# Half of the attention's statistics and transposes recorded with the convolutions, and copies by VectorE beside DMAs

## The chip, the cores and the metric

The kernel runs on one core of a Trainium2 chip. Its time is device microseconds of one execution, the median of several; lower is better. PE is TensorE, DVE VectorE, ACT ScalarE, POOL GpSimd, SP SyncE, which only issues DMAs. One more number goes with each run: the clock that was granted to TensorE, as a share of full speed.

## The reference

The input is x, 2048 positions of 512 channels in bfloat16. Four layers follow each other, each added to its input:

```
x = x + conv(layernorm(x))        # S4: one long filter per channel, made from A, B, C, log_dt; plus u * Dskip
x = x + attention(layernorm(x))   # 32 heads of 16; each position looks at 8 keys: its own and 7 earlier ones, 2 apart
x = x + conv(layernorm(x))        # the same filter
x = x + attention(layernorm(x))   # the same weights
```

The filter K[d, l] is the real part of a sum over 128 modes of C * exp(dt * A * l) * dt * B. The convolution is made with Fourier transforms of length 4096 and keeps the first 2048 outputs. The attention is x @ wqkv, logits against the 8 keys (masked before the start), softmax, a weighted sum of the 8 values, and wo.

## The kernel before

**X and its turned copy.** X stays in SBUF for the whole kernel as 128 partitions x 2 column halves x 16 rows x 256. Partition p, row j is position 16p + j; the column half (`h`, `cp`) is channels 0 to 255 or 256 to 511. A quarter `q` is four rows j. The attention's matmuls need channels on the partitions, so X is turned into XT (`turned_view(U)`, in the memory of U, which in the convolution layers holds the normalised input), in eight pieces: column half by quarter. A piece is turned by a DMA transpose from SP's queue or by eight PE transposes into `pt_x` and a copy on ACT or DVE (L1290, L1293, L1296).

**Statistics.** The attention's layer norm needs mean and variance of every row: DVE's `bn_stats` (L1348) on each half row of 256 elements, 32 a layer, into `pst`, then `bn_aggr` (L1352), joined per quarter, then ACT. Queries and keys are projected from XT without waiting for the statistics, whose scale enters later.

**Stages and orders.** There are four stages, each a `Plan`: the preparation, the filter and the first convolution (`kernel_and_first_conv`); the first attention (`b_layer`); the second convolution (`a_layer`); the second attention (`b_layer` again). A stage records its operations, each with an engine, a cost in us, its dependences and rings of buffers that it takes and drops. The cost plays no part at run time. `either` records several ways of doing one operation, for example a copy on ACT or on DVE. A list of numbers, `ORDERS[stage]`, worked out beforehand, says which way is taken and in which order all operations are issued:

```
order = [int(i) for i in ORDERS[Plan.turn].split()]
taken = {self.ops[i][2] for i in order}
```

Each engine works through its own share in that order, and waits by semaphores for other engines. An instruction that waits holds everything behind it on its engine.

**The first convolution.** Tables of powers of the modes (Xtab, Ytab) are built in 8 units by DVE (`table_ops`, L467 to L480), PE contracts them to the filter, and the filter (kind k) and the input (kind u) go through a Fourier transform in two steps, in four channel groups `dc` of 128 with four pieces `c` each. After the first step the spectrum Z is turned (`turn`: an SP DMA transpose into `zt`, or PE transposes into `pt` and an ACT copy, L912). After the second step, ACT's casts give sp_u and sp_k (L903). `swapped` makes a copy of sp_u with the two halves of the partitions exchanged, by two DMAs of 64 partitions x 1024 (L959), and `product` (`pa`, L966, DVE) multiplies sp_u and its exchanged copy by sp_k. `inverse` (`vp`, PE; `VT`) and `final` (`ps_y`, PE; X evacuated by ACT or DVE, L1006) go back, and add to X. sp_k is also stored to `kt_scratch` in DRAM for the second convolution.

**The second convolution** does the same for its input alone. `xc` is the spectrum; the filter comes back as `Kt`, a tile of 128 x 2 x 1024, whose two rows per partition are the partition's own and the one 64 away. `load` fills it by two DMAs of 64 x 2 x 1024, 256 KB each: those of dc 0 and 1 by POOL's queue, those of dc 2 and 3 by SP's (L1219). `pa` (L1169) multiplies both rows.

**The attention.** `start(q)` turns X and takes the statistics. `pair` and `qk` project queries and keys (`ps_qk`, L1409 and L1428; evacuated to qT, kT, L1433). `ahead` copies the last keys' columns to the front of kT (L1451) by SP's DMA, ACT or DVE. The products of queries and shifted keys are DVE's (L1508), the sums over a head are PE's (`Lp`, L1519). Then come softmax and, with the values (`ps_v`, L1463; VX), the products L1684, their sums on PE (L1700), and the output projection (`ps_o`, L1784) with X added.

Of the kernel before, what the change touches and what calls it, by code (L numbers as in the profile page):

```python
# [19 lines left out]
S = 2048  # L20
# [210 lines left out]
def load_params(nc, pp, prm):  # L231
# [307 lines left out]
def prepare(nc, pl, lp, pp, psA, psK, raw, identf, block, ones, M, cb, T, ln, X, D2, marks):  # L539
# [215 lines left out]
    marks["seeds"], marks["casts"] = o, casts  # L755


def kernel_and_first_conv(nc, tc, C, prm, x2d, const, kt_dram, eps, Wt):
    with ExitStack() as es:
        mt = es.enter_context(tc.tile_pool(name="k_mt", bufs=1))  # L760
        M = Multipliers(mt)
# [1200 lines left out]
```

## Time and profile before

| | |
|---|---|
| median of 3 runs | 442.48 us (439.23 to 443.36) |
| the profiled execution | 438.31 us, of which the span from first to last instruction is 436.5 us |
| mean granted TensorE clock | 0.986 |
| first convolution, with tables and filter | 0 to 165 us of the span |
| first attention | to about 276 us |
| second convolution | to about 326 us |
| second attention | to 436.5 us |

The stages overlap by a few microseconds at their borders. Busy times are sums of one engine's instructions in a stretch of the span. In the rows by group, the number ahead of the comma is the total busy time, the one behind it the mean duration of one instruction, then the idle time of that engine just before, and what ended it.

### The profile page before, as it was taken

What the parts mean: (1) busy time and instruction counts of PE and PEld (TensorE: products, weight loads), DVE (VectorE), ACT (ScalarE), POOL (GpSimd) and SP (SyncE); (2) the same over time, 40 slices, a digit from 0 to 9 for tenths busy, and PEclk for the clock granted to TensorE, in tenths of its full rate; (3) what the DMA queues carried; (4) which work ended last, traced back from release to release, by engine and by line L of the source; (5) the groups of instructions that cost most, each with busy time, mean ns of one, the idle gap of its engine ahead of it and who ended that gap; (6) DMA issues with size and microseconds to landing.
All of it is one profiled execution on the core that took longest, in us unless ns stands there. A gap on an engine that the chain in (4) does not pass through costs nothing.

```text
span 436.5 us, 11533 instructions
## 1 busy us (share of the span) xinstructions
PE 373.6 (86%) x4773; PEld 233.7 (54%) x4810; DVE 395.3 (91%) x659; ACT 320.6 (73%) x523; POOL 31.6 (7%) x94
## 2 busy tenths in 40 slices
PE   1376877788799988999997899898979999998995
PEld 1242665675587764446643344577754336743452
DVE  6999999799989479999899999998779999999994
ACT  6899999599789774677842578998855588853331
POOL 1000000000000410010000520010000010000150
PEclk9999899899899999999999999999999999999999
DMA  8977197789939988011213597299982000223296
GB/s 223 188 207 259 63 186 163 138 164 192 172 70 191 184 210 170 12 38 47 76 49 72 123 228 133 40 185 222 203 151 50 36 2 2 83 85 63 43 156 173
DMA packets 107306, 55.13 MB, mean 126 GB/s; under 512 B 85341, under 2 KB 97774, under 8 KB 106998
## 3 DMA queue, kind: packets, MB, share of 16 engines
q1 hardware_dynamic: 103990, 49.08, 53.4%
q0 software_dynamic: 2976, 5.06, 6.1%
q8 instruction: 37, 0.61, 0.6%
q10 hardware_dynamic: 288, 0.26, 0.2%
q14 instruction: 15, 0.12, 0.1%
HBM read 20.34 MB, written 6.29 MB: 61 GB/s over the span
## 4 chain that ended last, share of the span: by engine, by line
PE 38%; DVE 13%; DMA 6%; issue 2%; ACT 2%; SPq 0%; DVEq 0%; ACTq 0%
PE po L1700 7%; PE ps_qk L1409 6%; PE ps_v L1463 6%; PE ps_qk L1428 6%; DVE prod L1684 4%; PE Lp L1519 4%; PE ps_o L1784 3%; DVE prod L1508 2%; DMA oT<-ot 2%; DMA zt<-Z 2%; DMA Kt<-kt_scratch 2%; DVE pa L1169 1%; PE vp L1181 1%; PE ps_y L1202 1%; DVE ln_st_a L199 1%
## 5 line engine op out<-in xcount | busy, mean ns | idle before, releaser
L1684 DVE TENSOR_TENSOR prod<-VX,L 128x512 bf16<-128x512 bf16 (+2 forms) x72 | 75.5, 1102 | 2.0 <-ACT VX L1474 1.0
L1508 DVE TENSOR_TENSOR prod<-qT,kT 128x4096 bf16<-128x4096 bf16 (+1 forms) x40 | 72.1, 1861 | 1.8 <-ACT kT L1451 1.0
L1700 PE MATMUL po<-prod,sb_ident 128*128 128x512 bf16 x233 | 56.4, 379 | 2.8 <-DVE prod L1684 2.0
L1700 PEld LDWEIGHTS <-sb_ident 128*128 128x128 bf16 x240 | 23.1, 98 | 31.3 <-issue 4.1
L1463 PE MATMUL ps_v<-wv,U 128*128 128x256 bf16 x256 | 31.4, 273 | 0.6 <-ACT VX L1474 0.3
L1784 PE MATMUL ps_o<-wo_t,oT 128*128 128x512 bf16 x124 | 31.4, 379 | 0.4 <-ACT oT L1733 0.2
L875 ACT CAST Z<-ps_s 128x1024 bf16<-128x1024 f32 (+1 forms) x36 | 31.6, 952 | 0.0
L1474 ACT ACTIVATE VX<-ps_v,rs 128x256 bf16<-128x256 f32 x64 | 26.8, 474 | 6.0 <-PE ps_v L1463 5.6
L1409 PE MATMUL ps_qk<-U,wqk 128*128 128x512 bf16 x128 | 30.6, 380 | 0.3 <-ACT L L1647 0.3
L1718 ACT CAST ot<-po 128x1024 bf16<-128x1024 f32 (+1 forms) x16 | 15.1, 959 | 20.6 <-PE po L1700 20.6
L1428 PE MATMUL ps_qk<-U,wqk 128*128 128x512 bf16 x128 | 29.3, 379 | 0.0
L1463 PEld LDWEIGHTS <-U 128*128 128x128 bf16 x256 | 24.3, 98 | 8.9 <-issue 3.1
L966 DVE TENSOR_TENSOR pa<-sp_u,sp_k 128x2048 bf16<-128x2048 bf16 x16 | 19.6, 1222 | 7.9 <-DMA sp_u<-sp_u 4.3
L1519 PE MATMUL Lp<-prod,sb_bones 128*32 128x512 bf16 x256 | 22.9, 383 | 2.7 <-DVE prod L1508 2.7
L1348 DVE BATCH_NORM_STATS2 pst<-X 128x6 f32<-128x256 bf16 x64 | 21.9, 412 | 3.5 <-DMA sb_minus<-c_minus 2.6
L1169 DVE TENSOR_TENSOR pa<-xc,Kt 128x2048 bf16<-128x2048 bf16 x16 | 19.3, 1220 | 6.1 <-DMA Kt<-kt_scratch 4.1
L1409 PEld LDWEIGHTS <-wqk 128*128 128x128 bf16 x128 | 11.8, 98 | 16.8 <-issue 3.6
L1428 PEld LDWEIGHTS <-wqk 128*128 128x128 bf16 x128 | 12.2, 98 | 15.4 <-issue 1.6
L1784 PEld LDWEIGHTS <-oT 128*128 128x128 bf16 x128 | 12.2, 98 | 15.0 <-ACT oT L1733 0.7
L892 PE MATMUL xp<-zt,sb_C 128*128 128x512 bf16 x45 | 16.1, 411 | 4.3 <-DMA zt<-Z 1.4
L872 PE MATMUL ps_s<-KT,FK 128*128 128x128 bf16 (+1 forms) x360 | 18.3, 209 | 1.0 <-ACT KT L845 0.6
L1181 PE MATMUL vp<-sb_IC,pa 128*128 128x128 bf16 x256 | 16.3, 219 | 3.0 <-DVE pa L1169 2.7
(221 smaller groups left out, 841.3 us busy)
## 6 DMA issues: line engine op xcount, KB each, us to landing
sp_u<-sp_u SPq DMA_DIRECT2D x32, 128.0 KB, 3.0
kt_scratch<-sp_k SPq DMA_DIRECT2D x16, 256.0 KB, 3.9
Kt<-kt_scratch POOLq DMA_DIRECT2D x16, 256.0 KB, 7.7
Kt<-kt_scratch SPq DMA_DIRECT2D x16, 256.0 KB, 5.3
X<-in_A_u_dram SPq DMA_DIRECT2D x8, 256.0 KB, 5.6
X<-in_A_u_dram SPq DMA_DIRECT2D x4, 512.0 KB, 4.7
out_dram<-X SPq DMA_DIRECT2D x16, 128.0 KB, 2.0
VX<-VX SPq DMA_DIRECT2D x4, 448.0 KB, 3.7
```

Source lines behind the costliest of these rows:

```text
L875: nc.scalar.copy(box["Z", kind, dc, b0][:, 0:n // 4, :, jq * 16:(jq + 1) * 16].rearrange("p g r k -> p r g k"), box.pop(("s1", kind, dc, j ...
L1169: nc.vector.tensor_tensor(pr[:], x[:].unsqueeze(1).to_broadcast([128, 2, 1024]), box.pop(("kt", dc, c))[:], ALU.mult)
L1348: nc.vector.bn_stats(pst[:, j, cp, :], X[:, cp, j, :])
L1409: nc.tensor.matmul(ps[:], wqk[:, ct, f0:f0 + 128], XT[:, ct // 2, 4 * s:4 * s + 4, ct % 2, :], start=(ct == 0), stop=(ct == 3))
L1428: nc.tensor.matmul(box[name][:, k * 512:k * 512 + 512], wqk[:, ct, f0:f0 + 128], XT[:, ct // 2, 4 * s:4 * s + 4, ct % 2, :], start=(ct == ...
L1463: nc.tensor.matmul(ps[:, jj].rearrange("p t h d -> p (t h d)"), XT[:, ct // 2, j + jj, ct % 2, :], wv[:, ct, fp * 256:(fp + 1) * 256], sta ...
L1474: nc.scalar.activation(out, ps, ACT.Identity, scale=r)
L1508: nc.vector.tensor_tensor(pr[:], windows(q, 0, 2), windows(kT[fp][:, a:a + n2, col(w):col(w) + 1024], -DIL * 128, 2), ALU.mult)
L1519: nc.tensor.matmul(Lp[r0:r0 + 32, w // 4, :], bones[:, w % 4 + k, :], pr[:, k, f2 - a, hb * 512:(hb + 1) * 512], start=(n == 1 and k == 0) ...
L1684: nc.vector.tensor_tensor(p2[:].rearrange("p w j t d h -> p w (j t) d h"), windows(v, -DIL * 256, taps), l.to_broadcast([128, taps, nj * 2 ...
L1700: nc.tensor.matmul(po[:, c:c + 512], ident[:], p2[:, t, k + j:k + j + 2].rearrange("p j t d h -> p (j t d h)"), start=first, stop=stop)
L1784: nc.tensor.matmul(ps, oT[:, ft // 2, o:o + 128], wo_t[:, ft, :], start=(ft == 0 and not res), stop=(ft == 3))
```

## The change

- **Half 0 ahead.** A new function `ahead`, recorded at the end of both convolutions, turns column half 0 of X and takes its 16 half statistics within the convolution's plan. `start` of the attention keeps half 1. The other ways of making statistics (which the orders before did not take) are gone. U and `pst` are now allocated from the start, and the table X lies in U's memory until the contraction of unit 6 is done, so the transposes of half 0 in the first convolution wait for that.
- **Exchanged halves.** `swapped` may use two DVE copies of 64 partitions x 1024 instead of two DMAs. The new order takes them for 7 of the 16: (dc, c) = (0,2), (1,0), (2,0) and all of dc 3.
- **Kt copies.** `load` of dc 2 and 3 may fetch each row once, by two DMAs of 128 KB, and let DVE copy the other half of the tile, two copies of 64 x 1024. Taken for 7 of the 8, all but (3,1).
- **Turned spectra.** The copy of `pt` into `zt` may be DVE's too. Taken for five pieces in the second convolution.
- **Orders anew.** All four lists are replaced, so other ways are taken elsewhere as well. Over the kernel, DVE's instructions go from 661 to 689: 14 exchange copies and 14 Kt copies of 64 x 1024, 5 copies into zt and 3 more key copies are added; 3 casts of xc, 2 copies of pt_x, 3 subtractions on L and one addition on the value weights go. The DMAs in SP's queue go from 210 to 194. All eight pieces of half 0 are turned by SP's DMAs in the two convolutions; in the first attention two pieces of half 1 go by SP's DMA, one by ACT and one by DVE; in the second three by SP's DMA and one by ACT.

The core of the diff (orders and passed arguments left out):

```diff
-    def __init__(self, nc, tc, es, M):
+    def __init__(self, nc, tc, es, M, room):
...
-        self.X = pool.tile([128, UNIT, 2, NX, 2], BF, name="Xtab")
+        self.X = room[:].rearrange("p j d -> p (j d)").rearrange("n (h c e t) -> n h c e t", h=UNIT, c=2, e=NX)
...
+def ahead(pl, nc, X, XT, pst, psA, ident, ready, free, loaded):
...
+        def dma(js=js):
+            nc.sync.dma_start(XT[:, 0, js].rearrange("c j t p -> c (j t) p"), X[:, 0, js].rearrange("p j c -> p (j c)"), transpose=True)
...
+        pl.mark(("xt", q), pl.either(("turned", q), lambda: pl.op("S", 1.4, dma, ready[q], free, lag=3.2),
+                                     lambda: by_pe("A", 0.92, nc.scalar.copy), lambda: by_pe("V", 1.13, nc.vector.tensor_copy)))
+        pl.mark(("hs", q), *[pl.op("V", 0.34, lambda j=j: nc.vector.bn_stats(pst[:, j, 0, :], X[:, 0, j, :]), ready[q])
+                             for j in range(q * 4, q * 4 + 4)])
...
         def swapped(dc, c):
-            def swap():
+            def swap(move):
                 s = box["u", dc, c]
                 t = box["swap", dc, c] = box["xs"].pop(0)
                 for h in range(2):
-                    nc.sync.dma_start(box["U"][64 * h:64 * h + 64, t], box["U"][64 - 64 * h:128 - 64 * h, s])
...
+                    move(box["U"][64 * h:64 * h + 64, t], box["U"][64 - 64 * h:128 - 64 * h, s])
...
+                def once():
+                    k = box["kt", dc, c] = kp.tile([128, 2, 1024], BF, name="Kt", tag="Kt")
+                    for h in range(2):
+                        nc.sync.dma_start(k[64 * h:64 * h + 64, h], kt_dram[dc, c, 64 * h:64 * h + 64])
+
+                def other():
+                    k = box["kt", dc, c]
+                    for h in range(2):
+                        nc.vector.tensor_copy(k[64 - 64 * h:128 - 64 * h, h], k[64 * h:64 * h + 64, h])
...
+        ahead(pl, nc, X, turned_view(U), pst, psA, ident, [Xq[0, q] for q in range(4)], prev, [])
...
-            both = [turn(cp) for cp in range(2)]
-            ready = [r for r, _ in both]
-            turned[q] = [t for _, t in both]
...
+            turned[q] = [pl.outer(("xt", q)), turn()]
+
+            def half_stats(j):
+                nc.vector.bn_stats(pst[:, j, 1, :], X[:, 1, j, :])
```

More of the change, by code (lines that the diff above doesn't have):

```diff
@@ L755, in prepare, with mm, back_in, by_pe @@
     marks["seeds"], marks["casts"] = o, casts
-def kernel_and_first_conv(nc, tc, C, prm, x2d, const, kt_dram, eps, Wt):
+def ahead(pl, nc, X, XT, pst, psA, ident, ready, free, loaded):
+    box = {}
+    for q in range(4):
+        js = slice(q * 4, q * 4 + 4)
+        def dma(js=js):
+            nc.sync.dma_start(XT[:, 0, js].rearrange("c j t p -> c (j t) p"), X[:, 0, js].rearrange("p j c -> p (j c)"), transpose=True)
+        def mm(q=q):
+            pt = box[q] = psA.tile([128, 8, 128], BF, name="pt_x", tag="psA")
+            for k in range(8):
+                nc.tensor.transpose(pt[:, k, :], X[:, 0, q * 4 + k // 2, k % 2 * 128:k % 2 * 128 + 128], ident[:])
+        def back_in(copy, q=q, js=js):
+            copy(XT[:, 0, js], box.pop(q)[:].rearrange("c (j t) p -> c j t p", j=4))
+        def by_pe(eng, us, copy, q=q, mm=mm, back_in=back_in):
+            key = ("psA", "x", q)
+            return pl.op(eng, us, lambda: back_in(copy), free, pl.op("P", 0.5, mm, ready[q], loaded, take=key), drop=key)
+        pl.mark(("xt", q), pl.either(("turned", q), lambda: pl.op("S", 1.4, dma, ready[q], free, lag=3.2),
+                                     lambda: by_pe("A", 0.92, nc.scalar.copy), lambda: by_pe("V", 1.13, nc.vector.tensor_copy)))
+        pl.mark(("hs", q), *[pl.op("V", 0.34, lambda j=j: nc.vector.bn_stats(pst[:, j, 0, :], X[:, 0, j, :]), ready[q])
+                             for j in range(q * 4, q * 4 + 4)])
+def kernel_and_first_conv(nc, tc, C, prm, x2d, const, kt_dram, eps, Wt, U, pst):
     with ExitStack() as es:
@@ L1087, in kernel_and_first_conv, with a_layer @@
                     u_fft(dc + 1)
+                if dc == 1:
+                    ready = [list(Xq[0, q]) for q in range(4)]
+        ahead(pl, nc, X, turned_view(U), pst, psA, ident, ready, Cd[6], L["ident"])
         pl.run()
     return X
-def a_layer(nc, tc, C, X, kt_dram, U):
+def a_layer(nc, tc, C, X, kt_dram, U, pst):
     with ExitStack() as es:
@@ L1222, in load @@
             else:
-                Kl[dc, c] = pl.op("S", 1.15, lambda: go(nc.sync), take=("kt", dc, c), lag=4.0)
+                def once():
[6 more added lines that the diff above has]
+                        nc.vector.tensor_copy(k[64 - 64 * h:128 - 64 * h, h], k[64 * h:64 * h + 64, h])
+                Kl[dc, c] = pl.either(("load", dc, c), lambda: pl.op("S", 1.15, lambda: go(nc.sync), take=("kt", dc, c), lag=4.0),
+                                      lambda: pl.op("V", 0.84, other, pl.op("S", 1.15, once, take=("kt", dc, c), lag=3.5)))
         for dc in range(4):
@@ L1237, in a_layer, with b_layer @@
                 final(dc, k, nj)
+        ahead(pl, nc, X, turned_view(U), pst, psA, ident, [Xq[0, q] for q in range(4)], prev, [])
         pl.run()
-def b_layer(nc, tc, C, X, Wt, VX, XT, eps, ln, center, evac, done, VSTAT_Q):
+def b_layer(nc, tc, C, X, Wt, VX, XT, pst, eps, ln, center, evac, done, VSTAT_Q):
     with ExitStack() as es:
@@ L1304, in start @@
-            ready = [r for r, _ in both]
-            turned[q] = [t for _, t in both]
-            def sums():
-                ps = box["sum", q] = psA.tile([128, 4], F32, name="ps_sum", tag="psA")
-                for j in range(j0, j1):
-                    for ct in range(4):
-                        nc.tensor.matmul(ps[:, j - j0:j - j0 + 1], XT[:, ct // 2, j, ct % 2, :], mones[:, 0:1],
-                                         start=(ct == 0), stop=(ct == 3), skip_group_check=True)
-            def square(j):
-                nc.scalar.activation(halves(oT[:, j // 8, j % 8 * D:j % 8 * D + D]), X[:, :, j, :], ACT.Square, bias=nm[:, j:j + 1], accum_out=rs[:, NV + j:NV + j + 1])
@@ L1317, in root @@
-            def root():
-                r = rs[:, NV + j0:NV + j1]
-                nc.scalar.activation(nm[:, js], r, ACT.Ln, bias=eps[:, 0:1], scale=1.0 / D)
-                nc.scalar.activation(r, nm[:, js], ACT.Exp, scale=-0.5)
-            def by_sums():
-                key = ("psA", "sum", q)
-                a = pl.op("P", 0.9, sums, turned[q], Wd.get("k", []), take=key)
-                a = pl.op("V", 0.1, lambda: nc.vector.tensor_copy(nm[:, js], box.pop(("sum", q))[:]), a, drop=key)
-                a = [pl.op("A", 0.72, lambda j=j: square(j), a) for j in range(j0, j1)]
-                return pl.op("A", 0.5, root, a)
@@ new lines, in summed, with normed, square, norm @@
+    def summed(j, ps):
+        if j // 4 not in BN_Q:
+            nc.scalar.activation(X[:, :, j, :], halves(ps), ACT.Identity, accum_out=ln.sum[:, j:j + 1])
+        else:
+            nc.scalar.copy(X[:, :, j, :], halves(ps))
+    def normed(pl, q, after):
+        j0, j1 = q * 4, q * 4 + 4
+        def square(j):
+            nc.scalar.activation(halves(U[:, j, :]), X[:, :, j, :], ACT.Square, bias=ln.nm[:, j:j + 1],
+                                 accum_out=ln.sq[:, j:j + 1])
+        def norm(j):
+            nc.scalar.activation(halves(U[:, j, :]), X[:, :, j, :], ACT.Identity, bias=ln.nb[:, j:j + 1],
+                                 scale=ln.rstd[:, j:j + 1])
+        if q in BN_Q:
+            for k in (j0, j0 + 2):
+                o = [pl.op("V", 0.6, lambda j=j: ln.gather(X, 0, j, j + 1), after[j - j0]) for j in (k, k + 1)]
+                o = [pl.op("V", 0.09, lambda j=j: ln.gathered(j, j + 1), o[j - k]) for j in (k, k + 1)]
+                o = pl.op("A", 0.2, lambda k=k: ln.root(k, k + 2), *o)
+                o = pl.op("V", 0.08, lambda k=k: ln.offset(k, k + 2), o)
+                for j in (k, k + 1):
+                    pl.mark(("u", j), pl.either(("norm2", j), lambda: pl.op("V", 0.32, lambda j=j: ln.norm(halves(U[:, j, :]), X[:, :, j, :], j), o),
+                                                lambda: pl.op("A", 0.71, lambda j=j: norm(j), o)))
+            return
+        o = pl.op("V", 0.12, lambda: nc.vector.tensor_scalar(ln.nm[:, j0:j1], ln.sum[:, j0:j1], -1.0 / D, None, ALU.mult),
+                  *after)
+        o = [pl.op("A", 0.62, lambda j=j: square(j), o) for j in range(j0, j1)]
+        o = pl.op("A", 0.2, lambda: ln.root_of_squares(j0, j1), *o)
+        o = pl.op("V", 0.09, lambda: ln.offset_by(j0, j1), o)
+        for j in range(j0, j1):
+            a = pl.either(("norm2", j), lambda: pl.op("A", 0.71, lambda j=j: norm(j), o),
+                          lambda: pl.op("V", 0.32, lambda j=j: ln.norm(halves(U[:, j, :]), X[:, :, j, :], j), o))
+            pl.mark(("u", j), a)
@@ L1935, with stored @@
+    def stored(pl, q, after):
+        for j, a in enumerate(after, q * 4):
+            pl.op("S", 0.45, lambda j=j: nc.sync.dma_start(ov[:, j, :].rearrange("p (h c) -> p h c", h=2), X[:, :, j, :]), a, lag=2.2)
+    b_layer(nc, tc, C, X, Wt, VX, turned_view(U), pst, eps, ln, True, summed, normed, BN_Q)
+    a_layer(nc, tc, C, X, kt_dram, U, pst)
+    b_layer(nc, tc, C, X, Wt, VX, turned_view(U), pst, eps, ln, False, lambda j, ps: nc.scalar.copy(X[:, :, j, :], halves(ps)), stored, range(4))
 _INS = ['A_u', 'A_A_re', 'A_A_im', 'A_B_re', 'A_B_im', 'A_C_re', 'A_C_im', 'A_log_dt', 'A_Dskip', 'B_x', 'B_wqkv', 'B_wo']
```

122 lines of the change are left out of this document (31 added, 91 removed), and 119 rows, old and new, of the table ORDERS.

## The prediction

> **What bounds the kernel now.** I read the page's table of engines first, then the stretches of the span, one for each stage, then the groups, the chain and the timeline where a stretch was not full.
>
> ```profile
> PE 373.6 (86%) x4773; PEld 233.7 (54%) x4810; DVE 395.3 (91%) x659; ACT 320.6 (73%) x523; POOL 31.6 (7%) x94
> ```
>
> VectorE (DVE) carries the most, 395.3 us of 436.5, and the change gives it more. So the question is where its 41 idle microseconds lie. The next view has the span in seven stretches: first convolution (0 to 165), first attention (to 276, the third stretch running 2 us over), second convolution (to 326), second attention. The columns are PE, PEld, DVE, ACT and POOL busy, then clock, DMA share and GB/s.
>
> ```profile
> 0.00:165.00 165.00, 122.45 (x2830) 94.33 (x2851) 143.66 (x313) 144.54 (x204) 8.21 (x12) 0.97 0.83 174
> 165.00:232.00 67.00, 66.03 (x458) 35.01 (x460) 64.33 (x88) 43.19 (x87) 3.01 (x27) 1.00 0.27 68
> 232.00:278.00 46.00, 40.66 (x254) 19.40 (x257) 45.27 (x81) 31.03 (x70) 8.63 (x17) 1.00 0.58 121
> 278.00:326.00 48.00, 41.79 (x567) 33.97 (x571) 40.70 (x47) 41.70 (x49) 1.19 (x2) 1.00 0.95 177
> 326.00:342.00 16.00, 15.74 (x84) 7.20 (x85) 14.26 (x44) 9.76 (x18) 0.00 (x0) 1.00 0.29 62
> 342.00:392.00 50.00, 49.63 (x393) 26.63 (x392) 49.13 (x39) 35.27 (x76) 3.03 (x27) 1.00 0.14 42
> 392.00:436.50 44.50, 37.32 (x200) 17.17 (x196) 38.00 (x53) 15.12 (x23) 7.53 (x9) 0.98 0.56 107
> ```
>
> DVE is idle 21.3 us in the first convolution, 2.7 and 0.7 in the first attention, 7.3 in the second convolution, 1.7, 0.9 and 6.5 in the second attention. So in the attentions DVE is full and TensorE (PE) nearly so; the convolutions have room on DVE, and the second one is short of DMA (share 0.95). The change moves DVE work from the full stages to those with room.
>
> Cut finer, at the end of the first convolution, the start of each attention and the end of the second convolution:
>
> ```profile
> 141.70:165.00 23.30, 19.40 (x436) 16.22 (x439) 13.54 (x19) 17.89 (x25) 6.07 (x1) 1.00 0.92 196
> 165.00:177.50 12.50, 12.46 (x70) 6.18 (x70) 11.38 (x46) 5.93 (x10) 0.00 (x0) 1.00 0.65 139
> 177.50:231.00 53.50, 52.57 (x386) 28.39 (x386) 51.95 (x42) 37.26 (x78) 3.01 (x27) 1.00 0.17 49
> 231.00:241.10 10.10, 7.42 (x60) 3.21 (x62) 10.10 (x6) 2.56 (x4) 0.00 (x0) 1.00 0.24 46
> 304.40:319.20 14.80, 13.20 (x188) 10.95 (x187) 10.57 (x9) 12.40 (x14) 0.00 (x0) 1.00 1.10 209
> 326.20:336.70 10.50, 10.47 (x55) 5.01 (x55) 8.91 (x39) 5.40 (x9) 0.00 (x0) 1.00 0.40 76
> ```
>
> Both attentions open on PE alone (12.46 of 12.50; 10.47 of 10.50): the first product of queries and keys waits for projections, not for the statistics beside them.
>
> The price list, from the page's groups and from single lines asked for one by one (these give minimum/median/maximum ns):
>
> ```profile
> L966 DVE TENSOR_TENSOR pa<-sp_u,sp_k 128x2048 bf16<-128x2048 bf16 x16 | 19.6, 1222 | 7.9 <-DMA sp_u<-sp_u 4.3
> ...
> L1348 DVE BATCH_NORM_STATS2 pst<-X 128x6 f32<-128x256 bf16 x64 | 21.9, 412 | 3.5 <-DMA sb_minus<-c_minus 2.6
> L1169 DVE TENSOR_TENSOR pa<-xc,Kt 128x2048 bf16<-128x2048 bf16 x16 | 19.3, 1220 | 6.1 <-DMA Kt<-kt_scratch 4.1
> ```
> ```profile
> L1293 DVE COPY U<-pt_x x3: 672/673/692, 166.0 to 326.9; 128x1024 bf16<-128x1024 bf16 x3
> L1451 DVE COPY kT<-kT x2: 317/340/363, 170.2 to 176.0; 128x768 bf16<-128x768 bf16 x2
> L1160 DVE CAST xc<-xp x6: 1216/1217/1220, 285.9 to 305.6; 128x1024 bf16<-128x1024 f32 x6
> L1042 DVE TENSOR_TENSOR wv<-wv,wm x1: 1217/1217/1217, 54.3 to 54.3; 128x2048 bf16<-128x2048 bf16 x1
> ```
>
> One half-row statistic lasts 0.41 us but 64 fill 21.9 us, so a train of them costs 0.34 each; neighbours overlap by 0.07 us.
>
> **The new operation's price.** No row of before shows a copy of 64 partitions x 1024 from one half of the partitions to the other. From below: the key copy of 768 elements inside SBUF, 0.34 us. From above: the copy of 1024 elements out of PSUM, 0.67. I take 0.45, the lower row scaled by its elements (0.34 x 1024/768), because the new copy stays in SBUF too. 28 of them are 12.6 us, bounds 9.5 and 18.8.
>
> [...]
>
> **First convolution.** DVE gains 14 copies (7 of 16 exchanges of halves), 6.3 us; 16 half statistics, 5.5; it loses one addition on the value weights, 1.2: +10.6 (bounds +9.1 and +13.7). The other trades with ScalarE (normalised rows, small casts) nearly cancel. By the new order 6 copies and one statistic, less that addition, stand ahead of the last table operation at 141.7 (+1.8); 15 statistics and 8 copies, 5.1 + 3.6 = 8.7 us, stand behind it. There DVE has 23.30 - 13.54 = 9.8 us free. So the tail holds them if they fit the gaps, and what opens the gaps is partly the exchange itself: 4.3 of the 7.9 us idle before the products L966 end with sp_u's DMA, which lands 3.0 us after its issue.
>
> ```profile
> sp_u<-sp_u SPq DMA_DIRECT2D x32, 128.0 KB, 3.0
> ...
> Kt<-kt_scratch SPq DMA_DIRECT2D x16, 256.0 KB, 5.3
> ```
>
> Two copies at 0.9 us replace that landing at 7 of the 16 places. Against this stand the +1.8 ahead of the tables, and the new transposes of half 0 in SP's queue, one of them ahead of the last turn of the kernel spectrum, which the last products wait for:
>
> ```profile
> 161.70 8.15 SPq L1296 DMA_TRANSPOSE U<-X  x6
> ```
>
> That is 1.4 us of queue for each. It waits for the unit 6 table's last reader, since the table X now lies in that memory; that reader is done before the tail. Gains of up to 4.3 against 1.8 + 1.4 = 3.2 of losses: **0**, bounds -4 and +10.6 (every added microsecond on the path).
>
> **First attention.** 16 statistics (5.5 us) leave, and one copy from PSUM. That does nothing by itself in the opening, which is PE's. But the new order puts fewer projections ahead of the first product: 36 matmuls behind two turns, where there were 48. A matmul is 6.04/28 = 0.216 us by the chain:
>
> ```profile
> 165.04 1.05 PE pt_x L1290 x16
> ...
> 171.27 6.04 PE ps_qk L1428 x28
> ...
> 312.45 6.66 DMA Kt<-kt_scratch
> ```
>
> 12 x 0.216 = 2.6 us earlier than the first product of before, here the start of this row:
>
> ```profile
> 177.53 6.91 DVE L1508 TENSOR_TENSOR prod<-qT,kT 128x2048 bf16<-128x2048 bf16 x6 [0.54 <-ACT kT L1433]
> ```
>
> In before the 32 statistics just about filled these 12.5 us (DVE 11.38); at 9.9 us they would have been late, so taking 16 away is what allows the new order. Behind the first product DVE sets the pace (51.95 of 53.50, then 10.10 of 10.10). There it gets three key copies, 1.0, four aggregations, 0.4, and two casts of 1024 elements (2.4), and is rid of a cast of 1024 and smaller additions (about 3.0, by the cast's 1.22 per 1024): +0.9. Together **-1.7**; bounds -4 (the whole of the statistics' 5.5 less what PE's 66.03 of 67 forbids) and +1.
>
> **Second convolution.** Seven of the eight Kt tiles loaded by SP come once (2 x 128 KB) instead of twice; 14 copies of 0.45 make the other half, 6.3 us. DVE also evacuates five turned spectra (3.4 by the PSUM copy) and is rid of three xc casts (3.7) and some of the values' casts. The stretch before 304.4 and the waits after it decide:
>
> ```profile
> 276.00:304.40 28.40, 25.07 (x332) 20.12 (x336) 26.24 (x33) 27.23 (x36) 1.19 (x2) 1.00 0.85 160
> ```
> ```profile
> 312.03 2.58 DVE L1169 TENSOR_TENSOR pa<-xc,Kt 128x2048 bf16<-128x2048 bf16 x2 [1.82 <-DMA Kt<-kt_scratch]
> ...
> 316.90 1.23 DVE L1169 TENSOR_TENSOR pa<-xc,Kt 128x2048 bf16<-128x2048 bf16 x1 [1.16 <-DMA Kt<-kt_scratch]
> ```
>
> With a third one after it the waits for Kt are 4.1 us (L1169's row), the chain runs through the last load (312.45), and DMA stands at 1.10 share and 209 GB/s. The 1.8 MB fewer would take some 9 us at that rate. Between 304.4 and 319.2 eight copies and three statistics come (4.6), one xc cast and two value casts go (3.7): DVE 10.57 + 0.9 = 11.5 of 14.8, so by DVE 3.3 could go; PE's 13.20 leaves 1.6. Ahead of it, DVE's net +1.6 fits into 28.4 - 26.2 = 2.2 of room. I take **-2**, a little past PE's margin since PE has 3 more idle earlier; bounds -4 and +3 (copies at 0.67 behind a landing that stays 5.3). In the tail behind it 11 half statistics ran before the change already, in gaps, so the thirteen of the new order there are nearly a swap:
> ```profile
> L1348 DVE BATCH_NORM_STATS2 pst<-X x11: 408/411/427, 321.6 to 325.9; 128x6 f32<-128x256 bf16 x11
> ```
>
> **Second attention.** The opening stays PE's; the first key copy goes from ScalarE to DVE, about 0.5 sooner. Behind, DVE takes some 3 us more of casts and additions from ScalarE, mostly in the last stretch, where it has 6.5 us free. **-0.5**, bounds -2 and +3.
>
> **Sum.** 0 - 1.7 - 2 - 0.5 = -4.2 against the profiled execution, 436.5 of span and 1.8 us outside it, 438.3: 434.1. The median of the runs is 442.48, 1.0095 of that execution; on its scale **438.2**.
>
> **Rivals.**
> *VectorE becomes the bound of the first convolution (slower).* The engine runs in order. A statistic or copy that waits for ScalarE's X or spectrum holds every table operation and product behind it, and the idle 21.3 us are not where the new work is. For it: only 9.8 us are free in the tail for 8.7, and the work before it had gaps of waits, not slack. Against it: sp_u's waits go. Price: the whole +10.6, with the gains of the other stages kept: 438.3 + 10.6 - 4.2 = 444.7, x 1.0095 = 449. It decides from about half the added work on the path.
> *PE keeps the gains.* In the first attention PE is 66.03 of 67, so earlier products only wait later for PE; in the second convolution the copies eat the DMA's gain. Then 0 all over: 442.5. For it: the stretch 177.5 to 231 has 0.9 us of PE idle. Against it: 231 to 241, where PE has 2.7 idle and waits for DVE's products.
> *The waits go entirely.* sp_u's 4.3 us leave the first convolution's end: 434.1 - 4.3 = 429.8, on the median's scale 433.9. For it: they are the largest releaser before L966. Against it: the other 3.6 of those 7.9 us end with something else, which can take their place.
> [...]
>
> **How the numbers follow.** Forecast 0.40, with its own range 435 to 441, half of it under 438.06, which is faster by over 1%, about what a measurement here can tell from no change. Waits gone 0.20; PE keeps 0.10; copies alone 0.08; VectorE the bound 0.22. Faster: 0.20 + 0.20 = 0.40. Same: 0.20 + 0.10 + 0.08 = 0.38. Slower: 0.22. The range runs from 432, below the case of waits gone, to 448, which leaves out about half of the slow case and little at the lower end.
>
> **What would show it.** Right: the first attention's opening transposes start within 2 us of 165, its first product about 10 us later, no wait for Kt over 0.5 us in the second convolution, whose end comes 4 us sooner, and 64 x 1024 copies of 0.4 to 0.5 us. Wrong: a first convolution that ends past 168, with DVE still idle for 18 us or more there; copies of 0.67; an interval from the last X of the first convolution to the first product that stays 12.5 us; products on DVE that end idle on PE.

## The result and the profile after

The change made the kernel slower: 460.06 us, median of 4 runs (459.29 to 460.94), against 442.23 before (439.23 to 443.36). The ratio is 1.044, 95% interval 1.039 to 1.049. The forecast was 438.2, the range 432 to 448.

The profiled execution took 459.29 us, its span is 457.5, against 438.31 and 436.5. The page's first table shows DVE with 15.2 us more than before (395.3). That is less than the 21 us by which the span grew, and 5.9 of it are one copy that was held up, as shown below:

```profile
PE 383.0 (84%) x4854; PEld 236.9 (52%) x4854; DVE 410.5 (90%) x687; ACT 319.5 (70%) x518; POOL 28.1 (6%) x91
```

The span falls into six stretches at the same events in both kernels: the first transpose or projection of an attention on PE, its first product of queries and keys on DVE, the first matmul of the second convolution. So each attention has an *opening*, up to its first product, and a *rest* behind it. The columns are those of the prediction: PE, PEld, DVE, ACT and POOL busy, clock, DMA share, GB/s. First the kernel before, then the one after:

```profile
0.00:165.04 165.04, 122.46 (x2831) 94.33 (x2851) 143.70 (x313) 144.54 (x204) 8.21 (x12) 0.97 0.83 174
165.04:177.53 12.49, 12.49 (x70) 6.18 (x70) 11.34 (x46) 5.96 (x10) 0.00 (x0) 1.00 0.65 139
177.53:276.08 98.55, 92.62 (x621) 46.90 (x624) 96.34 (x114) 66.40 (x143) 11.64 (x44) 1.00 0.38 85
276.08:326.67 50.59, 43.80 (x594) 35.74 (x600) 42.88 (x55) 43.73 (x54) 1.19 (x2) 1.00 0.91 170
326.67:336.73 10.06, 10.06 (x50) 4.59 (x48) 8.81 (x38) 5.43 (x9) 0.00 (x0) 1.00 0.36 69
336.73:436.50 99.77, 92.20 (x616) 45.97 (x618) 92.28 (x95) 54.54 (x106) 10.56 (x36) 0.99 0.32 70
```
```profile
0.00:170.60 170.60, 127.48 (x2866) 95.38 (x2867) 157.68 (x337) 145.16 (x202) 8.38 (x12) 0.93 0.77 162
170.60:180.50 9.90, 9.87 (x58) 4.99 (x58) 6.17 (x27) 5.23 (x8) 0.00 (x0) 1.00 0.22 41
180.50:297.20 116.70, 98.21 (x643) 48.46 (x641) 97.70 (x124) 67.21 (x149) 10.43 (x42) 0.94 0.37 69
297.20:345.80 48.60, 44.23 (x609) 36.23 (x609) 46.57 (x70) 45.61 (x53) 2.39 (x4) 1.00 0.79 140
345.80:355.70 9.90, 9.90 (x52) 4.70 (x52) 7.23 (x34) 6.48 (x13) 0.00 (x0) 1.00 0.55 88
355.70:457.50 101.80, 93.29 (x631) 47.11 (x629) 95.12 (x97) 49.80 (x96) 6.89 (x33) 1.00 0.29 65
```

Two stretches lose: the first convolution (165.0 to 170.6, +5.6) and the first attention behind its first product (98.6 to 116.7, +18.1). The second convolution wins 2.0 and the opening of the first attention 2.6. The last stretch loses 2.0. The lower granted clock of the first stretch (0.93 against 0.97) is not what lengthened it: in a run below (wo fetched early) it is 0.93 too, and the stretch ends at 165.0.

**The first convolution.** In the timeline of DVE, the two exchange copies of (3,0) fill 6.71 us where a pair fills 0.86 elsewhere; one of the two lasts 6.28. POOL's timeline has one long instruction at that place, the clearing of the first rows of VX:

```profile
147.56 6.71 DVE L985 COPY sp_u<-sp_u 64x1024 bf16<-64x1024 bf16 x2
154.30 0.43 DVE L780 BATCH_NORM_STATS2 pst<-X 128x6 f32<-128x256 bf16 x1
```
```profile
147.74 6.25 POOL L1797 MEMSET VX<- 1x7168 bf16 x1 [144.65 <-PE ps_s L898]
```

The copies end 0.28 us after the memset. Behind them stand a product, which ends at 155.85, then ScalarE, which starts its next spectrum 0.08 us later, and PE, which waits for that spectrum. The profile names no releaser for ScalarE's 5.48 us; that it waits for a buffer which the product frees is a reading of the code. The rows of ACT and PE:

```profile
155.93 1.01 ACT L929 CAST sp_k<-xp 128x1024 bf16<-128x1024 f32 x1 [5.48 <-issue]
```
```profile
156.99 0.82 PE L934 MATMUL pt<-sb_ident,Z 128*128 128x128 bf16 x8 [5.00 <-ACT sp_k L929]
```

The kernel before has the same memset at the same place, with no such copy beside it:

```profile
148.34 6.07 POOL L1805 MEMSET VX<- 1x7168 bf16 x1 [145.23 <-PE ps_s L872]
```

**The first attention.** While POOL issues twelve Kt loads of 256 KB (241.5 to 254.8), SP issues three transposes of the attention's output, at 242.73, 247.13 and 248.97. The first lands after 10.7 us; for the other two the trace has no landing. Timelines of SP and POOL:

```profile
247.13 12.43 SPq L1715 DMA_TRANSPOSE oT<-ot  x2
248.97 10.59 SPq L1715 DMA_TRANSPOSE oT<-ot  x1
```
```profile
241.46 4.77 POOL L1250 DMA_DIRECT2D Kt<-kt_scratch  x8
246.39 0.60 POOL L1250 DMA_DIRECT2D Kt<-kt_scratch  x1 [0.17 <-issue]
247.94 0.60 POOL L1250 DMA_DIRECT2D Kt<-kt_scratch  x1 [0.94 <-DMA Kt<-kt_scratch]
```

(The second row is the second transpose of the first row alone.) PE, in its order, waits until 267.13 in the output projection that needs them. The sixteen matmuls behind it then run without a wait, so they were ready. DVE, in turn, waits for PE to free the products' buffers:

```profile
253.48 0.61 PE L1776 MATMUL ps_o<-wo_t,oT 128*128 128x512 bf16 x2 [0.25 <-DMA oT<-ot]
267.13 1.03 PE L1776 MATMUL ps_o<-wo_t,oT 128*128 128x512 bf16 x2 [13.05 <-DMA oT<-ot]
267.95 4.57 PE L1692 MATMUL po<-prod,sb_ident 128*128 128x512 bf16 x16
```
```profile
270.84 0.69 DVE L1676 TENSOR_TENSOR prod<-VX,L 128x1024 bf16<-128x1024 bf16 x1 [11.32 <-PE po L1692]
```

Right behind each of the two stalls the clock was lower. From 156 to 160 the granted clock is 0.66, from 267 to 270 it is 0.52, and the sixteen matmuls above take 4.57 us, where sixteen of the same take 3.82 in a run below without this stall.

So the reading before the experiments was: two stalls, one of about 6 us and one of about 13, neither of them the duration of the added work. Each has its rival below.

### The profile page after: what moved, and what is told of

It reads as the page before. It is cut to its first block, busy times and chain, and to the rows that moved or that the text cites. A ratio compares the mean times of both kernels' runs of the same rounds, so it can differ in the third digit from the quotient of the medians.

```text
span 457.5 us, 11617 instructions
## 1 busy us (share of the span) xinstructions
PE 383.0 (84%) x4854; PEld 236.9 (52%) x4854; DVE 410.5 (90%) x687; ACT 319.5 (70%) x518; POOL 28.1 (6%) x91
## 3 DMA queue, kind: packets, MB, share of 16 engines
q1 hardware_dynamic: 100662, 44.75, 47.9%
## 5 line engine op out<-in xcount | busy, mean ns | idle before, releaser
L1676 DVE TENSOR_TENSOR prod<-VX,L 128x512 bf16<-128x512 bf16 (+2 forms) x72 | 76.0, 1101 | 15.5 <-PE po L1692 15.2
L1692 PE MATMUL po<-prod,sb_ident 128*128 128x512 bf16 x240 | 57.5, 384 | 5.2 <-DVE prod L1676 4.6
L1776 PE MATMUL ps_o<-wo_t,oT 128*128 128x512 bf16 x128 | 32.4, 383 | 13.6 <-DMA oT<-ot 13.3
L1710 ACT CAST ot<-po 128x1024 bf16<-128x1024 f32 (+1 forms) x15 | 13.7, 957 | 29.3 <-PE po L1692 29.2
L918 PE MATMUL xp<-zt,sb_C 128*128 128x512 bf16 x64 | 18.7, 381 | 4.4 <-ACT zt L938 4.0
L1511 PE MATMUL Lp<-prod,sb_bones 128*32 128x512 bf16 x256 | 21.1, 383 | 0.6 <-DVE prod L1500 0.5
L929 ACT CAST sp_k<-xp 128x1024 bf16<-128x1024 f32 x16 | 16.4, 1054 | 7.2 <-issue 6.9
L1883 ACT ACTIVATE X<-ps_o 128x512 bf16<-128x512 f32 x8 | 4.7, 594 | 21.3 <-PE ps_o L1776 21.3
```

The costliest lines, as they stand in the source:

```text
L1511: nc.tensor.matmul(Lp[r0:r0 + 32, w // 4, :], bones[:, w % 4 + k, :], pr[:, k, f2 - a, hb * 512:(hb + 1) * 512], start=(n == 1 and k == 0) ...
L1676: nc.vector.tensor_tensor(p2[:].rearrange("p w j t d h -> p w (j t) d h"), windows(v, -DIL * 256, taps), l.to_broadcast([128, taps, nj * 2 ...
L1692: nc.tensor.matmul(po[:, c:c + 512], ident[:], p2[:, t, k + j:k + j + 2].rearrange("p j t d h -> p (j t d h)"), start=first, stop=stop)
L1776: nc.tensor.matmul(ps, oT[:, ft // 2, o:o + 128], wo_t[:, ft, :], start=(ft == 0 and not res), stop=(ft == 3))
```

## The experiments

**The long copy.** GpSimd's memset goes behind the RR constants in its queue (it then runs at 186.9 to 193.0):

```diff
+ORDERS[1] = ORDERS[1].replace(" 0 ", " ", 1).replace(" 83 ", " 83 0 ", 1)
```

> The changed kernel, with GpSimd's clearing of VX (7168 elements, 6.25 us) moved behind the RR constants in its queue, so that it no longer runs at 147.7 to 154.0 us of the span. Theory: VectorE's copy inside SBUF cannot proceed while GpSimd writes; the one exchange copy that lasted 6.28 us (all others 0.42) was held by it. Then every exchange copy is 0.42 to 0.45 us, the first convolution ends about 5.5 us sooner (at 165 instead of 170.6), and the time is about 454.5 (453 to 456) against 460.1. Rival: the copy waits for something else there, the transposes of half 0 into U (first one issued at 148.3) or the load of X; then one copy of about 6 us stays and the time stays at 460.

Measured: 454.62 us (453.47 to 456.92), 5.4 less. In the profiled execution, the slowest of the four, the first convolution ends at 168.4 and not at 165; in later runs without the long memset it ends at 164.2 to 166.8. The exchange copies' line, minimum/median/maximum ns, in the kernel after and in this one:

```profile
L985 DVE COPY sp_u<-sp_u x14: 420/422/6279, 80.3 to 161.8; 64x1024 bf16<-64x1024 bf16 x14
```
```profile
L986 DVE COPY sp_u<-sp_u x14: 420/422/423, 81.3 to 159.3; 64x1024 bf16<-64x1024 bf16 x14
```

The transposes of half 0 and the load of X are still beside the copies, and no copy is long. That rival is out.

The other way round, the kernel before with four exchanges by DVE:

```diff
-                    nc.sync.dma_start(box["U"][64 * h:64 * h + 64, t], box["U"][64 - 64 * h:128 - 64 * h, s])
+                    (nc.vector.tensor_copy if dc == 3 else nc.sync.dma_start)(
+                        box["U"][64 * h:64 * h + 64, t], box["U"][64 - 64 * h:128 - 64 * h, s])
```

> The kernel before, with the four exchanges of halves of channel group 3 made by VectorE copies at the same places of the order, nothing else. GpSimd's clearing of VX runs there from 148.3 to 154.4 us of the span. Theory of the shared access: one copy that falls into that stretch lasts until its end (up to 6 us), and the first convolution ends 2 to 6 us later: 444 to 448 against 442. Rival: a copy costs 0.42 to 0.45 wherever it stands; all eight are that short and the time is 442 or a little less, as waits for sp_u's DMA go.

Measured: 445.52 us (2 runs), ratio 1.014 (1.003 to 1.025). The first convolution ends at 172.5, 7.5 us later, more than the 2 to 6 expected. One copy of 6.28 us appears where there was none:

```profile
L959 DVE COPY sp_u<-sp_u x8: 420/423/6280, 134.9 to 164.5; 64x1024 bf16<-64x1024 bf16 x8
```

Last, the memset at its old place, in 28 pieces:

```diff
-            Wl["VX"] = pl.op("G", 1.0, lambda: nc.gpsimd.memset(VX[0:1, :, 0:NV], 0.0))
+            Wl["VX"] = pl.op("G", 1.0, lambda: [nc.gpsimd.memset(VX[0:1, f, j], 0.0) for f in range(2) for j in range(NV)])
```

> The changed kernel, with GpSimd's clearing of VX at its place, but in 28 instructions of 256 elements instead of one of 7168. Theory: VectorE's copy waits for one GpSimd instruction at a time; between two small ones it gets through. Then the longest exchange copy is under 1 us, and the time about that with the clearing moved (454.6, 453 to 457). Rival: back-to-back writes of GpSimd keep the copy out as one long write did; a copy of 5 us or more stays, the time 458 to 461.

Measured: 456.50 us (454.10 to 457.71). The pieces last from 146.70 to 155.56, and the exchanges run among them, none over 0.52 us:

```profile
L985 DVE COPY sp_u<-sp_u x14: 420/424/519, 79.2 to 155.3; 64x1024 bf16<-64x1024 bf16 x14
```
```profile
146.70 8.86 POOL L1797 MEMSET VX<- 1x256 bf16 x28 [143.61 <-PE ps_s L898]
```
```profile
147.85 1.21 DVE L993 TENSOR_TENSOR pa<-sp_u,sp_k 128x2048 bf16<-128x2048 bf16 x1
```

So a copy did not wait here until GpSimd was idle: beside 28 pieces of 0.32 us each (8.86 in all) the longest took 0.52 us, 0.10 more than the median of 0.42. The product in that stretch (last row, 1.21 us against 1.22 elsewhere) is not held. Nor was it in the kernel before, beside the one long memset (148.34 to 154.41): a product that starts at 152.40 takes 1.22 us there. The long copy, 6.28 us, ended 0.28 us after the memset of 6.25 (154.27 and 153.99). Why a copy was held and a product was not, no trace shows.

**The wait for the turned output.** A tiny GpSimd copy reads the fourth turned piece ahead of the Kt loads in GpSimd's queue, so they wait for it. This is the gate:

```diff
+                if center and (fp, j) == (1, 4):
+                    nc.gpsimd.tensor_copy(gate[0:1, 0:1], oT[0:1, fp, j * 256:j * 256 + 1])
```

> The changed kernel, with one tiny GpSimd copy that reads the fourth turned piece of the attention's output (oT of head group 1, rows 4 to 7), ahead of GpSimd's loads of Kt; so the 256 KB loads begin only when that transpose has landed. Theory: the first attention lost its 15.5 us because two transposes (issued at 247.1 and 249.0) shared the DMA engines with twelve Kt loads and landed at 267; PE, in order, stood for 13 us behind them. Then the transposes land within 4 us, PE's wait for oT there is under 3 us, the first attention is about 10 us shorter, the time about 450 (447 to 453). Rival 1: the transposes are slow by themselves or wait for ot; then 460. Rival 2: the Kt loads, now later, stop the second convolution instead: the attention gains 10, the second convolution loses 5 or more, time 455 or above.

Measured: 446.42 us (446.12 to 446.95), 13.6 less, more than the 10 expected. The rest of the first attention takes 103.9 us. Waits of PE for this transpose in the first attention, in the kernel after and here (total, times):

```profile
  DMA oT<-ot: 13.3, 2
```
```profile
  DMA oT<-ot: 1.7, 2
```

Sixteen matmuls of the kind that took 4.57 us behind the stall, in this run:

```profile
254.31 3.82 PE L1693 MATMUL po<-prod,sb_ident 128*128 128x512 bf16 x16
```

The transposes are not slow by themselves (rival 1), and the second convolution does not pay (rival 2): it takes 48.2 us here.

> The changed kernel with both edits: GpSimd's clearing of VX later, and the Kt loads behind the fourth turned piece. Theory (two independent stalls): the gains add, 460.1 - 5.5 - 10 = 444.6 (441 to 448), about the kernel before. If one stall only hid the other, the time is above 448.

Measured: 440.51 us (439.82 to 442.88), ratio to the kernel before 1.003 (0.999 to 1.007). 5.4 and 13.6 make 19.0; together they are 19.5. So the gains add, within the spread of the runs: the kernel before, run again beside these, took 440.59, and by the ratios to it (1.044 after, then 1.035, 1.016 and 1.003) the gains are 0.9, 2.8 and 4.1%. The two stalls are the loss, and what is left of the change is worth nothing that can be measured. Its stretches:

```profile
0.00:166.78 166.78, 126.84 (x2849) 96.98 (x2868) 151.85 (x337) 145.05 (x202) 2.13 (x11) 0.97 0.77 165
166.78:176.65 9.87, 9.87 (x58) 5.00 (x58) 6.17 (x27) 5.24 (x8) 0.00 (x0) 1.00 0.29 57
176.65:279.83 103.18, 96.37 (x637) 48.05 (x640) 97.35 (x124) 67.46 (x149) 18.49 (x44) 1.00 0.33 78
279.83:327.74 47.91, 43.90 (x604) 36.32 (x609) 46.48 (x70) 45.59 (x53) 2.38 (x4) 1.00 0.81 141
327.74:337.73 9.99, 9.99 (x52) 4.73 (x52) 7.27 (x35) 6.51 (x13) 0.00 (x0) 1.00 0.55 88
337.73:439.50 101.77, 92.96 (x626) 47.12 (x629) 95.11 (x97) 49.77 (x95) 6.92 (x33) 0.99 0.29 65
```

First convolution +1.7, first opening -2.6, second convolution -2.7, but the rests of the attentions +4.6 and +2.0. The +1.7 is not clear of chance: the six runs with this same first convolution (memset late, both mended, and below wo early, late gate, old lists without and with the gate) end it at 164.5 to 168.4.

Most of the +4.6 can be read off PE's instructions. The rest holds 88 projections of queries and keys where there were 76: the 12 that left the opening are done here instead (12 x 0.216 = 2.6 us). And it holds 12 matmuls of the subtractions that left DVE (`ps_less`) where there were 4, 1.7 us. Together 4.3 us; PE's busy time there rose by 3.8. The next runs ask for more causes. First the fetch of wo, which stands in SP's queue ahead of most transposes, and the place of the gate:

```diff
+ORDERS[1] = ORDERS[1].replace(" 2 ", " ", 1).replace(" 1 ", " 1 2 ", 1)    # wo behind bones
-                if center and (fp, j) == (1, 4):
+                if center and (fp, j) == (0, 12):                              # late gate only
```

> The kernel with both stalls mended, with the fetch of wo (four DMAs of 128 KB, 2.55 us of SP's queue, at 236 us of the span, ahead of seven of the eight transposes of the attention's output) moved behind the fetch of bones, at about 172 us, where the kernel before has it. Theory: the first transposes land 2.5 us sooner, so that the gate opens sooner and PE and DVE save 1 to 2 us in the rest of the first attention (103.1 us against 98.6 before): 438.5 to 439.5 against 440.5. Rival: the rest of the first attention is longer because PE and DVE have more work in it (PE 96.3 busy against 92.7); then no change, 440 to 441.

> As with wo fetched early, and the gate of the Kt loads moved from the fourth to the sixth turned piece (head group 0, rows 12 to 15), so that only two transposes share the DMA engines with the loads. Theory: the last waits for oT in the first attention (13.2 us in all waits on oT's DMA over the kernel, 1.15 of them on PE at 268.6) go, another 1 to 2 us: 437 to 439. Rival: Kt now comes too late for the first products of the second convolution, which lose what the attention gains: 440 to 443.

Measured: 440.31 us (439.48 to 442.36) with wo early, no change: the rest of the first attention stays at 103.1. With the late gate 447.48 (446.17 to 449.05), 7 us worse, and not where the rival put it: the second convolution keeps its 47.9. The loads now start at 258.6 and meet the last transposes instead: PE waits for oT twice, 7.5 us, and the attention behind its first product takes 110.6:

```profile
174.41:284.97 110.56, 97.97 (x636) 48.78 (x640) 97.63 (x124) 67.14 (x148) 16.83 (x44) 0.98 0.33 68
```

In these runs the loads had to fall between two groups of transposes; the ill places cost 13 us (13.6 by the gate) and 7.

**The copies.** Exchanges by DMA again, in the mended kernel:

```diff
-                                          lambda: pl.op("V", 0.84, lambda: swap(nc.vector.tensor_copy), Pd["u", dc, c], take=("xs", dc, c)))
+                                          lambda: pl.op("V", 0.84, lambda: swap(nc.sync.dma_start), Pd["u", dc, c], take=("xs", dc, c)))
```

> The kernel with both stalls mended, with all 16 exchanges of halves by DMA again, at the same places of the order. What is left of the change: half 0 ahead, Kt loaded once, the new orders. Its first convolution ended at 166.8 against 165.0 before. Theory: the 14 copies are DVE work on the path (14 x 0.45 = 6.3 us, less what gaps hide), so without them the first convolution ends at 164 to 166 and the time is 438 to 440 against 440.5. Rival: the copies save waits for sp_u's DMA (4.3 us before the change), so without them the waits come back, the first convolution ends at 168 or later and the time is 442 to 445.

Measured: 447.72 us (447.26 to 449.60), 7.2 more than with the copies. The rival holds, and more strongly than stated: the first convolution ends at 175.4, and DVE's timeline has five waits for sp_u's DMA, 11.8 us together, the last two of them:

```profile
159.66 1.23 DVE L994 TENSOR_TENSOR pa<-sp_u,sp_k 128x2048 bf16<-128x2048 bf16 x1 [2.99 <-DMA sp_u<-sp_u]
...
166.39 2.36 DVE L994 TENSOR_TENSOR pa<-sp_u,sp_k 128x2048 bf16<-128x2048 bf16 x2 [4.04 <-DMA sp_u<-sp_u]
```

This order was made for the copies, so the 7 us are their worth in it and not against the kernel before, whose own order had 4.3 us of such waits.

The Kt copies alone, in the kernel before and in its order:

```diff
+                    if dc > 1 and (dc, c) != (3, 1):
+                        eng.dma_start(k[64 * h:64 * h + 64, h], kt_dram[dc, c, 64 * h:64 * h + 64])
+                        continue
...
+                if dc > 1 and (dc, c) != (3, 1):
+                    for h in range(2):
+                        nc.vector.tensor_copy(k[64 - 64 * h:128 - 64 * h, h], k[64 * h:64 * h + 64, h])
```

> The kernel before with one part of the change alone: seven of the eight Kt tiles of channel groups 2 and 3 come once from DRAM, and DVE copies the other half right ahead of the product that reads it; nothing else. Forecast of the prediction for the second convolution with this: 2 us shorter; here without the new order. Theory: the waits for Kt (4.1 us) shrink to under 1 and the copies (14 x 0.45 = 6.3) take their place in part, the second convolution is 0 to 2.5 us shorter, the time 438 to 441. Rival: copies directly ahead of the products are wholly on the path, the convolution is 2 to 4 us longer, time 443 to 445.

Measured: 440.99 us (437.78 to 442.59), ratio 1.000 (0.997 to 1.004). Its second convolution takes 51.6 us in this profile, against 50.6, which lies between the ranges of the theory and of the rival. DVE waits for no Kt load any more (4.1 us before), but the copies stand directly ahead of the products. This shows the price of a pair:

```profile
311.23 1.23 DVE L1173 TENSOR_TENSOR pa<-xc,Kt 128x2048 bf16<-128x2048 bf16 x1
312.37 1.22 DVE L1188 CAST VT<-vp 128x1024 bf16<-128x1024 f32 x1
313.62 0.87 DVE L1172 COPY Kt<-Kt 64x1024 bf16<-64x1024 bf16 x2
314.53 1.23 DVE L1173 TENSOR_TENSOR pa<-xc,Kt 128x2048 bf16<-128x2048 bf16 x1
```

From the cast's start to the second product's are 2.16 us; the first product and the cast, with nothing between, start 1.14 apart. So the pair costs 1.02 here, not 0.90: the copies start 0.03 us after the cast's end (313.59), and the product 0.04 after theirs (314.49), while the cast starts 0.09 before the end of the product ahead of it (312.46).

**The attention's orders.** The changed kernel with the lists of the kernel before for both attentions, the transposes and statistics of half 0 taken out of them, the memset late:

```diff
+ORDERS[1] = (    # the list of before, each number mapped to the same operation after, half 0 left out
...
+ORDERS[3] = (    # likewise
```

> The changed kernel with the lists of the kernel before for both attentions (each operation mapped to its number after the change; the transposes and statistics of half 0, now in the convolutions, left out) and GpSimd's clearing of VX late. The convolutions keep the changed orders with copies; no gate. With both stalls mended the changed kernel still spends 103.2 and 101.8 us behind the first products of the attentions, against 98.6 and 99.8 before. Theory: these 6.6 us, and the 13 us of oT, are the new lists' own, not the price of moving half 0. Then, with the old lists, openings are at most 12.5 and 10.1 us, the rests 98 to 99 and 99 to 100, the time 435 to 439 against 440.5 mended and 440 before. Rival: with half 0 taken out, the old order of the rest hits the Kt loads or PE in the same way; the rests stay above 102 and 101, the time 440 to 445.

Measured: 436.40 us (434.57 to 438.47, 12 runs), ratio to the kernel before 0.994 (0.991 to 0.997). This is 0.6% less than the kernel before, which took 439.98 beside it: a small gain, but clear of the spread. Its stretches:

```profile
0.00:165.00 165.00, 127.46 (x2866) 96.13 (x2867) 151.65 (x337) 145.18 (x202) 2.14 (x11) 0.98 0.78 167
165.00:177.50 12.50, 12.50 (x70) 6.18 (x70) 7.44 (x34) 5.97 (x10) 0.00 (x0) 1.00 0.37 88
177.50:277.47 99.97, 94.96 (x626) 48.11 (x625) 96.75 (x114) 66.40 (x143) 16.43 (x43) 0.97 0.34 78
277.47:325.66 48.19, 44.79 (x617) 36.90 (x616) 46.82 (x73) 45.90 (x55) 2.39 (x4) 1.00 0.83 142
325.66:335.72 10.06, 10.06 (x50) 4.59 (x48) 6.99 (x34) 5.43 (x9) 0.00 (x0) 1.00 0.48 59
335.72:435.50 99.78, 92.62 (x621) 45.94 (x618) 92.27 (x95) 54.54 (x106) 10.55 (x36) 0.99 0.34 70
```

The convolutions are the changed ones and give 0.0 and -2.4; the rests are back at 100.0 and 99.8. So 5.2 of the 6.6 us go with the new lists. But the gain of the first opening goes with them: it takes 12.5 us again, because PE fills it, though DVE is relieved from 11.3 to 7.4 us. Opening and rest of the first attention together are 111.0 us before, 113.1 with the new list and no stall, 112.5 with the old one: the new list moved work of PE from one side of the first product to the other, and saved nothing by it. In the second attention the new list costs 1.9 us. These single profiles differ by 1.0 us of span from the kernel before, less than the medians do (3.6), so the stretches do not say where all of the 0.6% comes from.

> The same with the gate of the Kt loads behind the fourth turned piece of the attention's output. Theory: in the old order that piece comes 12 us later relative to the loads, so the loads start late and collide with the last transposes or miss the first products of the second convolution: no gain or a loss, 437 to 444. Rival: the loads hurt the transposes in the old order too (one took 9.7 us in the chain of before), so the gate gains: 432 to 435.

Measured: 437.08 us (435.40 to 438.88), ratio 0.994 (0.991 to 0.998): no difference to the one without the gate. Its first attention's rest is 98.3, 1.7 shorter, its second convolution 49.2, 1.0 longer. The run decides little: in the old order the fourth piece is turned early, the gate opens at once, and the loads start at 246.6 instead of 245.8. That the piece would come 12 us later was wrong, so neither theory nor rival was tried.

## Why the prediction was wrong

*First convolution: forecast 0, measured +5.6.* The step that failed is the price of the new operation, 0.45 us wherever it stands. Thirteen of the fourteen copies cost about that (0.42), and one cost 6.28. The price was taken from rows of duration, with the order of DVE and what DVE waits for, and not from what runs beside it on GpSimd. POOL's 6.07 us at the end of that stage stand in the prediction's own table of stretches, and the row behind them, a memset at 148.34, right where the copies of dc 3 were to come, was left out of account. Without that stall the forecast held: with the memset out of the way the first convolution ended at 164.2 to 166.8 in six of the seven profiles, 168.4 in the other. DVE carries 8 us more there, less than the 10.6 worked out (9.1 at the least). The rival of VectorE as the bound, at 0.22, gave a slower time for a reason that did not occur; the added work found its gaps. So that the time came out slower does not speak for it.

*First attention: forecast -1.7, measured +15.6.* Its first half was right: 2.6 us less to the first product, 9.9 us. The step that failed came behind it. "DVE sets the pace" counted DVE's work there (+0.9; it is +1.0 in the mended kernel) and nothing of SP's queue against POOL's. Before, POOL issued its loads from 244.97 to 255.61 and SP no transpose between 243.69 and 255.82; in the new order three fell among the loads, and PE had its projection ahead of other work. The chain of the kernel before had these rows:

```profile
255.82 9.66 DMA oT<-ot
265.52 0.61 PE ps_o L1784 x2
```

That transpose was slow too, but PE had other matmuls meanwhile, and no wait of PE for oT shows in that attention. It was the sign that this wait was one reordering away from the path.

*Without the stalls* the rest of that attention was still 4.6 us longer. The prediction took the gain of the opening as a gain of the stage: it counted 12 projections fewer ahead of the first product and left out that PE does them behind it, and that the subtractions on L that left DVE go to PE. These are the 2.6 and 1.7 us above. The rival "PE keeps the gains" said this, and had 0.10: no change over all is what the mended kernel shows (1.003, with the convolution's gain used up in the attentions). Which of the matmuls are on the path was not tried.

*Second convolution: forecast -2, measured -2.0, and -2.4 to -2.7 in the mended kernels*, for the reasons given: DVE waits 0.6 us for Kt instead of 4.1 (none in the mended kernel), and its added work goes into its gaps. The row of the kernel after:

```profile
L1200 DVE TENSOR_TENSOR pa<-xc,Kt 128x2048 bf16<-128x2048 bf16 x16 | 19.1, 1222 | 1.2 <-DMA Kt<-kt_scratch 0.6
```

But the copies do not do it alone: in the old order (with all else as before) that convolution got no shorter. How much the new order adds was not separated, so the close agreement in size is in part luck.

*Second attention: forecast -0.5, measured +1.9.* The opening gained 0.2 of the 0.5; the rest is the new list again (99.8 with the old one). DVE's 2.8 us more there were foreseen, and that its idle time would take them was not borne out; what of them is on the path was not tried.

*Copies alone* has 0.08 among the chances. No run shows in the time what it would cost. What the runs showed is one pair at 1.02 us instead of 0.90; from it, 14 pairs are an estimated 1.7 us of DVE, 0.8 in each convolution.

## What to carry to other kernels

A copy that is moved from a DMA to VectorE must be checked against what GpSimd does in the same microseconds, above all one long memset; here both moving it and splitting it took the stall away (no copy over 0.42 and 0.52 us, where one had lasted 6.28). When orders change, look for transfers that were slow but covered: here a transpose of 9.7 us stood in the chain before with no wait of PE for it, and in the new order transposes of the same tile cost 13. Work taken from an engine gives nothing in a stretch that another engine fills: the statistics left the opening of the attention, and in the old order it took 12.5 us as before. And an event that comes sooner because work was put behind it is no gain of the stage: that work is still to be done.

## What the runs showed of the hardware

In the kernel after, the transposes into oT land in 3.2 us (median); the one issued at 242.73, while GpSimd's queue issued twelve loads of 256 KB (241.5 to 254.8), took 10.7 us, and the issue of another one, at 248.97, held SP's queue for 10.6 us. In the run with the late gate PE waited 4.38 and 3.10 us for such transposes. In the kernel after a one-partition memset of 7168 elements took GpSimd 6.25 us, and a VectorE copy inside SBUF lasted 6.28 us beside it instead of 0.42. A bfloat16 product of two tensors (1.22 us at 152.40) and a cast out of PSUM (1.22 at 153.55) beside that memset in the kernel before were not held, and half-row statistics (0.43 at 147.51) were not held beside its 28 pieces. Two copies between the halves of the partitions took 0.87 us at 313.62 in the kernel before with Kt loaded once, and overlapped neither with the cast ahead nor with the product behind; at 301.07 in the kernel after, the cast behind such a pair started 0.09 us before its end (301.86 and 301.95).
